# Last weight loads of a decode block in two pieces, with products of zeros ahead of TensorE's last pass

## The chip, the core and the metric

One core of one Trainium2 chip runs the whole kernel. The metric is the device time of one execution in microseconds. Weights come from HBM to SBUF by DMA, TensorE multiplies into PSUM, VectorE (DVE) and ScalarE (ACT) work on what TensorE leaves there, GpSimd (POOL) clears buffers, and SyncE (SP) issues the loads.

## The reference

One decode step for eight sequences of one token each, in f32: a pre-norm attention block over the last 1024 positions of a cache, then a gated feed-forward block, each with a residual.

```python
W  = min(4096, max(256, Sk // 4))                # 1024 of 4096 positions
q  = (layernorm(x) @ wq)                         # 8 x 4096, 32 heads of 128
s  = einsum(q, k_cache[last W]) * Dh ** -0.5     # 4 kv heads, each for 8 heads
o  = einsum(softmax(s), v_cache[last W]) @ wo
h  = x + o
g, u = layernorm(h) @ w_gate, layernorm(h) @ w_up    # 1024 x 3584 each
h2 = h + (gelu(g) * u) @ w_down                  # 3584 x 1024
```

Every weight is used once, so 111 MB are read for a result of 32 KB.

## The kernel before

**Tiles.** The activations are TensorE's stationary operand, 32 columns wide (eight tokens, each in every fourth column), and the weights stream past as the moving operand, 512 columns at a time. Four such products stand side by side in the four column groups of the array and write to four strips of 32 partitions in PSUM. `half(i, gates)` (L215) is one pass over a buffer: eight chunks `c`, each of four products (one per column group), the first four chunks into one half of `sums[i]`, the others into the other. A pass marks its middle and its end for the other engines.

**Buffers and loads.** There are two SBUF buffers of 8.4 MB. The twelve full loads (`units`, L151 to L156: wq, keys, values, wo, gate and up, two each) alternate between them, all on SP's queue, each issued when the pass that read the same buffer before it has ended. Then come the rest of `w_down` in row chunks of 128 rows (128 x 1024 f32, 0.52 MB each): 16 of them into buffer 0 in the pieces named by `PARTS` (L160, `wd0`, `wd1`, ...), three into buffer 1 by `ENDPARTS` (two, then one: the tails), and the last one as two blocks of columns by `ENDS` (160 and 96 of the 256 columns of a quarter: the ends).

**TensorE's order.** A loop of eight turns (L230) is written once. In a turn stand a pass `b` over buffer 1, two products with `y_sb` that fold four strips (L236; in most turns their result is not used), eight transposes of `source` (L241) that turn the last stage's result into the next stationary operand, and a pass `a` over buffer 0. Conditions leave out `b` in turns 1 and 4 and `a` in turn 3. Waits are counters that `take` lowers again (L209), so that the same code can wait in every turn: `go[0]` for a load and the operand of pass `a`, and `go_later` for gates inside pass `a`. GpSimd fills the gates' counters at the start with what the six earlier passes `a` will take (`GATE`, L197); in the last pass they hold it back for DVE's second operand (`go_0`, chunk 4) and for the later pieces of the loads (`go_1`, chunk 5; `go_2`, chunk 7). One chunk `c` of this last pass uses two row chunks.

**The end.** DVE adds the two halves of the last pass to the residual (`d1`, L423 and L424). TensorE then sums in PSUM's `acc`, by `quarters` (L427): the fold of pairs of strips (`add2` with `d1`) and the three row chunks of the tails (`chunk`, L434), in that order. ACT copies `acc` to `most` (L444). TensorE multiplies the two blocks of the last row chunk (L455), DVE adds each to `most` (`o_fin`, L458), and two DMAs write the result. Each engine works its queue strictly in the order written.

Of the kernel before, what the change touches and what calls it, by code (L numbers as in the profile page):

```python
# [7 lines left out]
P = 128  # L8
# [8 lines left out]
QW = D // NQ  # L17
N = 512
# [8 lines left out]
UNITS = 12  # L27
EARLY = 8
HEAD = 16
PARTS = (10, 4, 2)  # L30
ENDPARTS = (2, 1)
ENDS = (160, 96)
AHEAD = 3
PAD = 128


GATE = (1, 16, 16)
TURNS = 9
NO_B = (1, 4)
NO_A = (3,)  # L40


class Flow:
# [37 lines left out]
    def run(self, engine, make, *waits, mark=True, gives=None):  # L81
        ins = self.start(engine, make, waits)
        if gives is not None:
            ins.then_inc(*gives)
            return None
        if not mark:
            return None
        self.done[engine] += 1
        ins.then_inc(self.own[engine], 1)
        return self.own[engine], self.done[engine]  # L90
# [7 lines left out]
def decode_block(nc, x, units, dn, tails, ends, outs):  # L98

    fl = Flow(nc)  # L100
    run, move = fl.run, fl.move
    PE = nc.tensor
    scale = DH ** -0.5

    def sb(name, *shape):
        return nc.alloc_sbuf_tensor(name, list(shape), F32).ap()

    def bank(name, n):
        return nc.alloc_psum_tensor(name, [P, n], F32).ap()
# [5 lines left out]
    acc, fin = bank("acc", N), bank("fin", N)  # L115
# [3 lines left out]
    go = [fl.sem("go_a"), fl.sem("go_b")]  # L119
    go_later = [fl.sem(f"go_{i}") for i in range(len(GATE))]  # L120
    go_turn, go_fold = fl.sem("go_turn"), fl.sem("go_fold")
# [6 lines left out]
    for i in range(1, TURNS):  # L128
# [4 lines left out]
        nt += 1  # L133
        if i not in NO_A:
            seq += [("a", na, 0), ("a", na, 1)]
# [5 lines left out]
    def half_a(k, h=1):  # L141
        return at_mark["a", k, h]
# [8 lines left out]
    for u in range(UNITS):  # L151
        k, i = divmod(u, 2)
# [6 lines left out]
    q0 = EARLY  # L159
    for i, (n, sem) in enumerate(zip(PARTS, (go[0], *go_later[1:]))):  # L160
        c0 = (q0 - EARLY) * D
# [11 lines left out]
    last = q0  # L173
# [14 lines left out]
        pattern=[[-1, P]], channel_multiplier=1), z)  # L188
    y_sb = sb("y_sb", P, N)
    run("gpsimd", lambda e: e.memset(y_sb, 0.0), gives=(go_fold, 3))  # L190
    src_ok = run("gpsimd", lambda e: e.memset(source, 0.0))
    add2 = sb("add2", P, 2, 32)
    run("gpsimd", lambda e: e.tensor_add(
# [2 lines left out]
    for i, g in enumerate(go_later):  # L196
        run("gpsimd", lambda e: e.memset(note[:, i:i + 1], 0.0), gives=(g, GATE[i] * (passes - 1)))  # L197

# [10 lines left out]
    def take(sem, n):  # L209
        PE.wait_ge(sem, n).then_inc(sem, -n)  # L210

    def mark(ins):
        ins.then_inc(fl.own["tensor"], 1)

    def half(i, gates):  # L215
        gates = dict(gates)
        for c in range(NC):
            if c in gates:
                take(*gates[c])
            h = c // (NC // 2)  # L220
            for j in range(NQ):
                s = NQ * c + j
                ins = PE.matmul(  # L223
                    sums[i][32 * j:32 * j + 32, h * N:(h + 1) * N], still[i][:, 32 * s:32 * s + 32],
                    wbuf[i][:, s * N:(s + 1) * N],
                    start=(c % (NC // 2) == 0), stop=(c % (NC // 2) == NC // 2 - 1))
            if c % (NC // 2) == NC // 2 - 1:
                mark(ins)

    with PE.Fori(1, TURNS) as i:  # L230
        with PE.If(i != NO_B[0]):
            with PE.If(i != NO_B[1]):
                half(1, [(0, (go[1], 17))])
                take(go_fold, 1)
                for ch in range(2):
                    ins = PE.matmul(turned[0:32, ch * N:(ch + 1) * N], add2[:, ch, :], y_sb,  # L236
                                    start=True, stop=True)
                mark(ins)
        take(go_turn, 1)
        for n in range(NC):  # L240
            ins = PE.transpose(turned[:, n * P:(n + 1) * P], source[:, n * P:(n + 1) * P], ident)  # L241
        mark(ins)
        with PE.If(i != NO_A[0]):
            half(0, [(0, (go[0], 17)), *zip((4, 5, 7), zip(go_later, GATE))])
    fl.done["tensor"] = len(seq)


# [174 lines left out]
    d1 = sb("d1", P, N)  # L422
    tok = run("vector", lambda e: e.tensor_add(d1, rest, sums[0][:, 0:N]), tok, half_a(6, 0))  # L423
    d1_ok = run("vector", lambda e: e.tensor_add(d1, d1, sums[0][:, N:2 * N]), tok, half_a(6))  # L424


    def quarters(lhs, rhs, *waits, start=False, stop=False):  # L427
        for j in range(NQ):
            tok = run("tensor", lambda e: e.matmul(
                acc[32 * j:32 * j + 32, 0:QW], lhs(j), rhs(j), start=start, stop=stop),  # L430
                *waits, mark=(stop and j == NQ - 1))
        return tok

    def chunk(q, **flags):  # L434
        t, here = arrived[q]
        return quarters(lambda j: at[:, q, :], lambda j: t[:, j * QW:(j + 1) * QW], here, at_ok, **flags)

    quarters(lambda j: add2[:, j // 2, :], lambda j: d1[:, (j % 2) * QW:(j % 2) * QW + QW], d1_ok,
             start=True)
    chunk(last - 3)  # L440
    chunk(last - 2)
    tok = chunk(last - 1, stop=True)
    most = sb("most", P, QW)
    most_ok = run("scalar", lambda e: e.copy(most, acc[:, 0:QW]), tok)  # L444
# [8 lines left out]
    for (c0, n, t, here), d_ps in zip(blocks, (fin, sums[1])):  # L453
        for j in range(NQ):
            tok = run("tensor", lambda e: e.matmul(  # L455
                d_ps[32 * j:32 * j + 32, 0:n], at[:, last, :], t[:, j * n:(j + 1) * n],
                start=True, stop=True), here, d1_ok, mark=(j == NQ - 1))
# [103 lines left out]
```

## Time and profile before

| | |
|---|---|
| time, median of 3 runs | 263.79 us (263.63 to 263.81) |
| span of the profiled execution, first to last instruction | 262.3 us |
| median of the runs less this span | 1.5 us |
| TensorE busy | 138.9 us, 53% |
| DVE, ACT, POOL busy | 43.8, 13.5, 7.2 us |
| read from HBM | 111.18 MB, 424 GB/s over the span |
| packets on SP's load queue | 98.4% of the 16 DMA engines' span |

The profile gives no time of its own for that execution beside the span; the 1.5 us lie before the first and behind the last instruction. PE is TensorE, PEld its weight loads, which run beside the products. An f32 product stands in the trace as two records of PE, one behind the other. "PEq" means TensorE's own instruction sequencer, where the waits of `take` stand, so an idle time that ended with PEq includes waits for loads.

### The profile page before, as it was taken

The numbers are of one execution on the slowest core, as the hardware profiler recorded it, in microseconds if no ns is written. First come the engines' busy times: TensorE is split into PE (matmuls) and PEld (weight loads), VectorE is DVE, ScalarE is ACT, GpSimd is POOL, SyncE is SP. The second block draws the span as 40 slices with busy tenths as digits, with TensorE's granted clock in tenths as the row PEclk, the third lists the DMA queues.
The fourth block names the chain that finished last, engine by engine and source line by source line (L and its number), as shares of the span: only waits on it lengthen the run. The fifth ranks groups of instructions, "written<-read, shape, count | busy, mean of one in ns | idle before, by whom it ended". The sixth has DMA issues, their size and how long they took to land. (4 is left out here: it accounts for less than half of the span.)

```text
span 262.3 us, 2253 instructions
## 1 busy us (share of the span) xinstructions
PE 138.9 (53%) x968; PEld 43.5 (17%) x968; DVE 43.8 (17%) x115; ACT 13.5 (5%) x19; POOL 7.2 (3%) x18
## 2 busy tenths in 40 slices
PE   0025905916706937507908608629409809209985
PEld 0021201301102222102302102122102302002321
DVE  0340100240100140400410101263100300100422
ACT  1000000000030010000000200000300000200000
POOL 5000000100000000100100000000000000000000
PEclk9999965975975986965965957986966968957999
DMA  8998997999899799989979998997999999799895
GB/s 320 485 440 360 480 480 340 460 480 440 360 480 480 320 480 480 440 360 480 480 320 480 480 430 370 480 480 320 480 480 400 400 480 480 320 420 500 370 421 229
DMA packets 3040, 111.31 MB, mean 424 GB/s; under 512 B 472, under 2 KB 728, under 8 KB 992
## 3 DMA queue, kind: packets, MB, share of 16 engines
q1 hardware_dynamic: 2880, 111.23, 98.4%
q10 hardware_dynamic: 160, 0.08, 0.1%
HBM read 111.18 MB, written 0.13 MB: 424 GB/s over the span
## 5 line engine op out<-in xcount | busy, mean ns | idle before, releaser
L223 PE MATMUL sum<-w,still 128*32 128x512 f32 x832 | 115.7, 716 | 98.3 <-PEq L210 98.3
L223 PEld LDWEIGHTS sum<-w,still 128*32 128x32 f32 x832 | 31.9, 129 | 177.7 <-issue 177.7
L241 PE MATMUL turned<-ident,source 128*128 128x128 f32 x64 | 10.1, 310 | 21.1 <-PEq L210 21.1
L241 PEld LDWEIGHTS turned<-ident,source 128*128 128x128 f32 x64 | 8.0, 157 | 26.4 <-issue 26.4
L236 PE MATMUL turned<-y_sb,add 128*32 128x512 f32 x24 | 11.3, 592 | 0.9 <-PEq L210 0.9
L319 DVE TENSOR_REDUCE nmax<-sum 128x1 f32<-128x1024 f32 x2 | 2.4, 1224 | 30.1 <-PE sum L223 30.1
L394 DVE TENSOR_TENSOR up<-up,sum 128x512 f32<-128x512 f32 (+1 forms) x2 | 1.4, 686 | 36.3 <-PE sum L223 36.3
L290 DVE TENSOR_SCALAR q<-sum 128x512 f32<-128x512 f32 x2 | 1.4, 692 | 24.4 <-PE sum L223 24.4
L275 DVE COPY still<-turned 128x1024 f32<-128x1024 f32 x4 | 4.7, 1220 | 4.0 <-PE turned L241 4.0
L384 DVE TENSOR_TENSOR gate<-gate,sum 128x512 f32<-128x512 f32 (+1 forms) x2 | 1.4, 685 | 21.7 <-PE sum L223 21.7
L346 DVE SCALAR_TENSOR_TENSOR o<-sum,share,o 128x128 f32<-128x128 f32 x12 | 4.2, 351 | 4.2 <-PE sum L223 3.8
L343 DVE TENSOR_SCALAR o<-sum,share 128x128 f32<-128x128 f32 x2 | 0.7, 350 | 22.9 <-PE sum L223 22.9
L321 ACT ACT_TABLE_LOAD x1 | 1.3, 1283 | 59.4 <-DVE nmax L319 59.4
L236 PEld LDWEIGHTS turned<-y_sb,add 128*32 128x32 f32 x24 | 2.6, 110 | 8.7 <-issue 8.7
L350 POOL MEMSET still<- 128x1024 f32 x2 | 1.9, 951 | 76.0 <-PE sum L223 76.0
L362 DVE TENSOR_TENSOR y_sb<-y_sb,sum 128x512 f32<-128x512 f32 x1 | 0.7, 686 | 16.0 <-PE sum L223 16.0
L361 ACT COPY y_sb<-sum 128x512 f32<-128x512 f32 x1 | 0.6, 586 | 50.7 <-PE sum L223 50.7
L321 ACT ACTIVATE source<-sum,nmax 128x1024 f32<-128x1024 f32 x2 | 2.2, 1113 | 18.8 <-PE turned L241 18.8
L295 POOL MEMSET still<- 128x1024 f32 x2 | 1.9, 956 | 45.7 <-PE sum L223 45.7
L363 DVE TENSOR_TENSOR y_sb<-y_sb,sum 128x512 f32<-128x512 f32 x1 | 0.7, 689 | 14.1 <-PE sum L223 14.1
L306 DVE COPY still<-turned 128x16 f32<-128x16 f32 x32 | 2.7, 165 | 2.1 <-PE turned L241 2.1
L260 ACT ACT_TABLE_LOAD x2 | 2.6, 1283 | 3.0 <-POOL ident L186 2.9
(61 smaller groups left out, 38.8 us busy)
## 6 DMA issues: line engine op xcount, KB each, us to landing
w<-dn SPq DMA_DIRECT2D x1, 5120.0 KB, 22.9
w<-dn SPq DMA_DIRECT2D x1, 2048.0 KB, 27.4
w<-dn SPq DMA_DIRECT2D x1, 1024.0 KB, 29.4
w<-tails SPq DMA_DIRECT2D x1, 1024.0 KB, 12.8
w<-tails SPq DMA_DIRECT2D x1, 512.0 KB, 13.7
w<-ends SPq DMA_DIRECT2D x1, 320.0 KB, 14.1
w<-units SPq DMA_DIRECT2D x12, 29.5
w<-ends SPq DMA_DIRECT2D x1, 192.0 KB, 14.1
```

The source lines that it names most:

```text
L223: ins = PE.matmul(sums[i][32 * j:32 * j + 32, h * N:(h + 1) * N], still[i][:, 32 * s:32 * s + 32], wbuf[i][:, s * N:(s + 1) * N], start=(c ...
L236: ins = PE.matmul(turned[0:32, ch * N:(ch + 1) * N], add2[:, ch, :], y_sb, start=True, stop=True)
L241: ins = PE.transpose(turned[:, n * P:(n + 1) * P], source[:, n * P:(n + 1) * P], ident)
L260: tok = run("scalar", lambda e: e.activation(sd, ve, AF.Sqrt), tok)
L275: run("vector", lambda e: e.tensor_copy(still[i].rearrange("p (c j m) -> p c j m", c=NC, j=NQ), turned.rearrange("p (c m) -> p c m", c=NC) ...
L290: tok = run("vector", lambda e: e.tensor_scalar(q_sb, sums[hf][:, 0:N], scale, None, op0=ALU.mult), done(0, 0))
L295: cleared.append(run("gpsimd", lambda e: e.memset(still[hf], 0.0), done(0)))
L306: run("vector", lambda e: e.tensor_copy(to[:, :, b, s, a, REP * b:REP * b + REP].rearrange("p k (h i) -> p k h i", h=2), frm[:, s, a * HB ...
L319: tok = run("vector", lambda e: e.tensor_reduce(out=nmax, in_=sums[hf], axis=AX.X, op=ALU.max, negate=True), done(1))
L321: p_ok = run("scalar", lambda e: e.activation(source, sums[hf], AF.Exp, bias=nmax, accum_out=tot), tok, at_mark["t", 1 + hf])
L346: tok = run("vector", lambda e: e.scalar_tensor_tensor(out, o3[:, b], share[hf][:, b:b + 1], o_sb, op0=ALU.mult, op1=ALU.add), tok, done(2 ...
L350: cleared[hf] = run("gpsimd", lambda e: e.memset(still[hf], 0.0), done(2))
```

## The change

`PARTS` goes from (10, 4, 2) to (12, 4): the 16 row chunks come in two loads, the gates inside pass `a` are two and not three, and the second load is waited for at chunk 6 of the last pass. In the last turn, five products of a zeroed tile `idle` (128 x 32 by 128 x 512, into 32 partitions of the bank `fin`) stand between the transposes and pass `a`; GpSimd clears the tile at the start. Behind the loop, the fold of pairs stands behind the two row chunks of the first tail, no longer ahead of them.

```diff
-PARTS = (10, 4, 2)
+PARTS = (12, 4)
-GATE = (1, 16, 16)
+GATE = (1, 16)
+GATES = (4, PARTS[0] // 2)
+WARM = 5
...
+    idle = sb("idle", P, N)
+    run("gpsimd", lambda e: e.memset(idle, 0.0), mark=False)
     src_ok = run("gpsimd", lambda e: e.memset(source, 0.0))
...
         mark(ins)
+        with PE.If(i == TURNS - 1):
+            for _ in range(WARM):
+                PE.matmul(fin[0:32, 0:N], idle[:, 0:32], idle, start=True, stop=True)
         with PE.If(i != NO_A[0]):
-            half(0, [(0, (go[0], 17)), *zip((4, 5, 7), zip(go_later, GATE))])
+            half(0, [(0, (go[0], 17)), *zip(GATES, zip(go_later, GATE))])
...
-    quarters(lambda j: add2[:, j // 2, :], lambda j: d1[:, (j % 2) * QW:(j % 2) * QW + QW], d1_ok,
-             start=True)
-    chunk(last - 3)
+    chunk(last - 3, start=True)
     chunk(last - 2)
+    quarters(lambda j: add2[:, j // 2, :], lambda j: d1[:, (j % 2) * QW:(j % 2) * QW + QW], d1_ok)
     tok = chunk(last - 1, stop=True)
```

TensorE's instructions in the loop, from the transposes to the end of pass `a`, before (`x7` and the like count equal instructions; `go_a` is `go[0]`):

```order
L241 MATMUL turned<-ident,source 128x128 x7
L243 COMPARE_AND_BRANCH
L223 MATMUL sum<-w,still 32x512 [waits go_a_done]
L223 MATMUL sum<-w,still 32x512 x15
L223 MATMUL sum<-w,still 32x512 [waits go_0_done]
L223 MATMUL sum<-w,still 32x512 x3
L223 MATMUL sum<-w,still 32x512 [waits go_1_done]
L223 MATMUL sum<-w,still 32x512 x7
L223 MATMUL sum<-w,still 32x512 [waits go_2_done]
L223 MATMUL sum<-w,still 32x512 x3
```

The same place after the change (the lines of the code have moved by four and more):

```order
L245 MATMUL turned<-ident,source 128x128 x7
L247 COMPARE_AND_BRANCH
L249 MATMUL fin<-idle 32x512 x5
L247 UNCONDITIONAL_BRANCH
L250 COMPARE_AND_BRANCH
L227 MATMUL sum<-w,still 32x512 [waits go_a_done]
L227 MATMUL sum<-w,still 32x512 x15
L227 MATMUL sum<-w,still 32x512 [waits go_0_done]
L227 MATMUL sum<-w,still 32x512 x7
L227 MATMUL sum<-w,still 32x512 [waits go_1_done]
```

Five products and a condition now stand ahead of the wait for the first load; the wait at chunk 5 has moved to chunk 6 and the one at chunk 7 is gone.

TensorE behind the loop, before (`vector_done` is DVE's count, `we0` and `we1` the tails, `wl0` the first block of the ends):

```order
L429 MATMUL acc<-d,add 32x256 [waits vector_done]
L429 MATMUL acc<-d,add 32x256 x3
L429 MATMUL acc<-w,at 32x256 [waits we0_done]
L429 MATMUL acc<-w,at 32x256 x7
L429 MATMUL acc<-w,at 32x256 [waits we1_done]
L429 MATMUL acc<-w,at 32x256 x3
L455 MATMUL fin<-w,at 32x160 [waits wl0_done]
```

The same place after the change:

```order
L436 MATMUL acc<-w,at 32x256 [waits we0_done,vector_done]
L436 MATMUL acc<-w,at 32x256 x7
L436 MATMUL acc<-d,add 32x256 [waits vector_done]
L436 MATMUL acc<-d,add 32x256 x3
L436 MATMUL acc<-w,at 32x256 [waits we1_done]
L436 MATMUL acc<-w,at 32x256 x3
L461 MATMUL fin<-w,at 32x160 [waits wl0_done]
```

The fold with its wait for `d1` now stands between the two tails; the first tail's products carry a wait for an earlier DVE instruction, the copy to `at`.

## Rows read from the trace of the kernel before

**Rows 1.** Chain of waits that ended last: start, duration, what.
```profile
245.45 14.08 DMA w<-ends
...
260.47 0.25 DVE o_fin L458
```

**Rows 2.** Timeline of TensorE's products, last turn: start, duration, line, records, idle before.
```profile
235.55 8.99 PE L223 MATMUL sum<-w,still 128*32 128x512 f32 x64 [10.93 <-PEq L210]
244.35 1.88 PE L236 MATMUL turned<-y_sb,add 128*32 128x512 f32 x4
246.16 1.09 PE L241 MATMUL turned<-ident,source 128*128 128x128 f32 x8
247.67 4.50 PE L223 MATMUL sum<-w,still 128*32 128x512 f32 x40 [0.41 <-PEq L210]
252.57 1.92 PE L223 MATMUL sum<-w,still 128*32 128x512 f32 x16 [0.40 <-PEq L210]
255.05 1.06 PE L223 MATMUL sum<-w,still 128*32 128x512 f32 x8 [0.56 <-PEq L210]
256.92 0.64 PE L429 MATMUL acc<-d,add 128*32 128x256 f32 x8 [0.80 <-DVE d L424]
257.45 1.07 PE L429 MATMUL acc<-w,at 128*32 128x256 f32 x16
258.74 0.64 PE L429 MATMUL acc<-w,at 128*32 128x256 f32 x8 [0.21 <-DMA w<-tails]
259.57 0.48 PE L455 MATMUL fin<-w,at 128*32 128x160 f32 x8 [0.20 <-DMA w<-ends]
```

**Rows 3.** Timeline of DVE and ACT behind the last pass.
```profile
256.18 0.69 DVE L424 TENSOR_TENSOR d<-d,sum 128x512 f32<-128x512 f32 x1 [4.12 <-PE sum L223]
...
259.44 0.37 ACT L444 COPY most<-acc 128x256 f32<-128x256 f32 x1 [17.69 <-PE acc L429]
...
260.12 0.32 DVE L458 TENSOR_TENSOR o_fin<-most,fin 128x160 f32<-128x160 f32 x1 [1.19 <-PE fin L455]
260.47 0.25 DVE L458 TENSOR_TENSOR o_fin<-most,sum 128x96 f32<-128x96 f32 x1
```

**Rows 4.** Timeline of SP: the three loads of the 16 row chunks.
```profile
224.68 1.28 SPq L94 DMA_DIRECT2D w<-dn  x3
```

**Rows 5.** Costliest groups, the fold products: busy, mean ns of one, idle before.
```profile
L236 PE MATMUL turned<-y_sb,add 128*32 128x512 f32 x24 | 11.3, 592 | 0.9 <-PEq L210 0.9
```

**Rows 6.** Timeline of TensorE, an earlier turn: fold and transposes.
```profile
50.31 1.88 PE L236 MATMUL turned<-y_sb,add 128*32 128x512 f32 x4
52.13 1.09 PE L241 MATMUL turned<-ident,source 128*128 128x128 f32 x8
```

**Rows 7.** Timeline at the start: GpSimd's clearing, DVE's first use of `source`.
```profile
2.12 0.52 POOL L190 MEMSET y_sb<- 128x512 f32 x1
...
13.29 0.80 DVE L268 TENSOR_SCALAR source<-x_sb,ln_mv,ln_rs 32x1024 f32<-32x1024 f32 x1
```

**Rows 8.** Timeline of TensorE: three of its twelve full passes.
```profile
22.69 9.60 PE L223 MATMUL sum<-w,still 128*32 128x512 f32 x64 [6.51 <-PEq L210]
...
177.48 9.01 PE L223 MATMUL sum<-w,still 128*32 128x512 f32 x64 [1.47 <-PEq L210]
...
216.19 8.43 PE L223 MATMUL sum<-w,still 128*32 128x512 f32 x64 [7.06 <-PEq L210]
```

**Rows 9.** Windows: length, busy time (records) of PE, PEld, DVE, ACT, POOL; clock; DMA.
```profile
235.50:239.50 4.00, 3.95 (x20) 1.15 (x24) 0.00 (x0) 0.00 (x0) 0.00 (x0) 0.51 1.14 492
239.50:244.40 4.90, 4.90 (x49) 1.51 (x42) 0.00 (x0) 0.58 (x1) 0.00 (x0) 1.00 0.93 401
...
256.20:262.30 6.10, 3.07 (x48) 1.05 (x48) 1.36 (x6) 0.37 (x1) 0.00 (x0) 1.00 0.58 220
...
169.40:174.60 5.20, 0.28 (x3) 0.31 (x4) 4.26 (x10) 0.20 (x1) 0.00 (x0) 1.00 1.20 517
```

## What the change was expected to do

> **What bounds the kernel now.** I read the chain of waits first. It runs back from the last instruction through the ends of `w_down` and lasts from their issue at 245.45 until they land at 259.53; behind that come only TensorE's short products, DVE's two additions and the output [rows 1]. So the loads end last, not the arithmetic, and SP's queue is never empty: the three loads of the 16 row chunks are issued at 224.68 [rows 4], 23 us before the first of them is used.
>
> The second view is TensorE's timeline of the last turn [rows 2]. The last pass starts three times, at 247.67, 252.57 and 255.05, each time after a wait, because a load lands there. The starts give the stream's pace: four row chunks take 4.90 us and two take 2.48, so a row chunk costs 1.21 us and a transfer of its own 0.06. The tails follow in the same way at 257.45 and 258.74 and the first block of the ends at 259.57.
>
> The third view is what stands between the pass and the end on DVE and ACT [rows 3]. `d1` is added at 256.18, 1.13 us after the last chunk began; the fold starts 0.05 us after that addition. ACT's copy of `acc` runs from 259.44 to 259.81, and DVE's first `o_fin` waits until 260.12, for the last block's products. ACT's copy could end 0.26 us later (260.12 less 0.05 of handover less 259.81) before `o_fin` felt it. That is the slack of the arithmetic behind the loads, and it is small: only the copy's place decides it.
>
> **The change part by part.**
>
> *Two loads for three.* The bytes are the same. One transfer fewer is worth 0.06 us by the pace above, so tails and ends land 0.06 us earlier. SP issues two loads in place of three, 0.43 us less of 1.28 [rows 4], at a time when it has nothing else to do: nothing. The first load now holds twelve row chunks and lands two row chunks later, so the last pass can start at 247.67 + 2 x 1.21 = 250.09. The second is there at 255.05 - 0.06 = 254.99. A pass that began at 250.09 would need 0.86 us a chunk (below), reach chunk 6 at 255.24 and chunk 7 at 256.10, 1.05 us later than before.
>
> *Five products of zeros.* TensorE works in order, so they push the last pass back. Their nearest row is the fold: the same shape, 128 x 32 by 128 x 512 in f32, one column group, two records a product. Four records take 1.88 us, one lasts 0.592, so they follow each other every (1.88 - 0.592) / 3 = 0.429 us [rows 2, 5]. Ten records of zeros take 4.29 us. The ends of what is unknown are wide: a record cannot go much below the 0.136 us that one transpose of 128 columns takes on average (1.09 / 8, which makes 1.4 us for ten), and at TensorE's lower clock, at which a record takes twice as long, ten take 8.6 us. I take 4.29, because shape and clock agree with the row.
>
> They begin when the transposes leave the array. In an earlier turn the transposes, at 52.13, began 0.06 us before the modelled end of the fold at 52.19 [rows 6]; so here the zeros begin at 246.16 + 1.09 - 0.06 = 247.19 and the pass can begin at 251.48. Its load has been there since 250.09: the pass is 1.39 us late, and the loads don't start it any more.
>
> The pass itself: 40 records in 4.50 us are ten rounds of four, the last record again 0.59, so a round takes 0.43 and a chunk, two rounds, 0.86 [rows 2]. Chunk 6 begins at 256.64, long after its load at 254.99, and chunk 7 at 251.48 + 7 x 0.858 = 257.49, where it was 255.05: 2.44 us later.
>
> *The end of it.* `d1` starts 1.13 us behind, at 258.62, and ends at 259.31; the fold begins at 259.36. This is where its new place counts. TensorE has left the pass at 258.35 and does the two row chunks of the first tail (0.43 each, from 1.07 for two against 0.64 for one [rows 2]) while DVE adds: they end at 259.21, 0.15 before the fold can start. Ahead of them, the fold would have pushed all three row chunks back and cost another 0.86. Behind the fold, the last tail starts at 259.79; it landed an us before. ACT's copy starts 0.70 after it, as it did [rows 2, 3], at 260.49, and ends at 260.86; DVE's `o_fin` starts at 260.91 in place of 260.12. The blocks' products, 0.43 behind the tail at 260.22 and 0.55 long to `o_fin`, are ready before. The end moves by 0.79 us.
>
> *What costs nothing.* The cleared tile is a 0.52 us instruction on GpSimd like the one for `y_sb` [rows 7]; it pushes the clearing of `source` to about 4 us, and DVE first writes there at 13.29. Without that cover it would cost its 0.52. The added condition is read in every turn between transposes and pass `a`. The trace has no row for one; a condition's jump and a wait lie between fold and transposes, which shift by 0.10 against the fold's pace (50.31 + 4 x 0.429 = 52.03, then 52.13) [rows 6]. I take 0 for it, between 0 and 0.10 in each turn: before every pass TensorE waits, 1.47 us where it waits least [rows 8], and in the last turn the jump lies behind 4.29 us of queued zeros. The wait for the copy to `at` at the first tail is over ten us old when it is met.
>
> The sum is 263.79 + 0.79 = 264.58: the profiled execution's span is 262.3, the median of the runs lies 1.5 above, and I keep that distance.
>
> **The size that can move.** The chain starts from the pass over buffer 1 at 235.55, and the length of that pass depends on when TensorE's clock rises: in its first 4 us the granted clock is 0.51, the lower level of 1.2 GHz, and then 1.00, the upper one of 2.4 [rows 9]. Twelve passes of equal work last from 8.43 to 9.60 us [rows 8]; this one took 8.99 [rows 2]. Nothing ties it to that value in another execution. Before, that was hidden behind the load at 247.67; now it moves the end one for one: +0.79 becomes +0.23 to +1.40, that is 264.02 to 265.19.
>
> **The rivals.**
>
> *The stream still ends last: 263.73.* If the last pass begins by 251.48 - 0.79 = 250.69, the copy of `acc` is early enough, and only the 0.06 of the transfer is left. For it: three or four zeros would fit (247.19 + 4 x 0.858 = 250.62), so the count is just one too many; and a short pass over buffer 1 leaves only +0.23. Against it: five are written, and a record would have to take under 0.35 us where the fold's take 0.429. The Trainium skill (TensorE: Matmul & The Clock Gate, section Back-to-back issue gap) gives about 216 ns between isolated products of 512 columns at the upper clock; by that, an estimate, five zeros take 1.1 us, the pass starts with its load at 250.09, and the time is 263.73. The trace disagrees for f32 products of this shape, 0.86 us each, so I give that rule little.
>
> *The clock falls: 266.0 to 267.2.* If products of zeros in a quarter of the array did not hold the clock, the last pass would begin at the lower level like the one at 235.55. At the upper level a pass takes 15 x 0.43 + 0.59 = 7.04; the twelve took 8.43 to 9.60, so this adds 1.4 to 2.6 to 264.58. For it: the pass at 235.55 began at the lower level after a wait of 10.93 us [rows 2, 9]. Against it: it stayed at 1.00 to the end through the gaps of the last turn, and between 169.4 and 174.6, after nothing but a fold, with TensorE busy for 0.28 us of 5.2 [rows 9]. The Trainium skill (the same page, section Part 4: PE-mode transpose) says that transposes do not count as busy for the clock; if so the zeros, not the transposes, must hold it, and no run so far shows zeros alone.
>
> *Faster.* Every landing is 0.06 us earlier and no other work shrinks, so no row gives a gain beyond that.
>
> **How the numbers follow.** 0.2%, about what a measurement of this kernel can tell from no change, is 0.53 us: slower begins at 264.32. With the pass's length spread evenly over what the rows show, the shift lies over 0.53 in (1.40 - 0.53) / 1.17 = 74% of cases. I give 0.60 to TensorE's chain ending last and over that bound (264.58 the likeliest), 0.30 to an end inside it (the rest of that spread, shorter zeros, the stream), 0.06 to the fallen clock, 0.04 to a gain that no row shows. Slower 0.66, same 0.30, faster 0.04. The range for 8 in 10 runs from the stream's 263.7 to 265.3, a little over the longest pass.
>
> **What would show it.** In the profile after: ten records of zeros 0.43 apart from about 247.2; the last pass one piece without a wait from about 251.5, chunk 6 not waiting; `d1` near 258.6; the fold begun by DVE, not by a load; the chain of waits through TensorE, DVE and ACT's copy and no longer through the ends. If the zeros end by 250.7, or the last pass starts with its load, the sum is wrong and the stream decides; if the granted clock is under 1.00 behind 247, the third case holds. All times move with the length of the pass at 235.5, which is to be read first.

## The result, and the profile after

The changed kernel takes 265.08 us (median of 11 runs, 263.91 to 265.78) against 263.81 (11 runs, 263.58 to 264.18) for the kernel before: the ratio is 1.0040, 95% interval 1.0030 to 1.0049. It is 0.4% slower, twice the 0.2% at which the prediction let slower begin, and its runs lie 1.87 us apart where those of before lie 0.60 apart. The profiled execution has a span of 264.2 us; it took 265.47 us, 0.39 over the median.

The chain that ended last no longer has a load in it (start, duration, what); this answers to [rows 1].

```profile
235.99 9.57 PE sum L227 x64
245.57 1.69 PE turned L240 x4
247.26 1.02 PE turned L245 x8
248.28 3.98 PE fin L249 x9
...
252.69 6.25 PE sum L227 x60
...
259.56 1.94 PE acc L436 x26
261.50 0.02 issue
261.52 0.38 ACT most L450
```

It runs through TensorE from the pass over buffer 1 to the copy of `acc`, 26 us without one wait for a load. The timeline of TensorE's products shows the same pieces with their records, to be held against [rows 2].

```profile
248.21 4.05 PE L249 MATMUL fin<-idle 128*32 128x512 f32 x9
251.67 0.63 PE L227 MATMUL sum<-w,still 128*32 128x512 f32 x3
252.10 0.59 PE L249 MATMUL fin<-idle 128*32 128x512 f32 x1
252.13 7.00 PE L227 MATMUL sum<-w,still 128*32 128x512 f32 x60
258.56 0.61 PE L436 MATMUL acc<-w,at 128*32 128x256 f32 x6
258.96 0.59 PE L227 MATMUL sum<-w,still 128*32 128x512 f32 x1
259.39 1.03 PE L436 MATMUL acc<-w,at 128*32 128x256 f32 x10
260.38 0.64 PE L436 MATMUL acc<-d,add 128*32 128x256 f32 x8
260.84 0.61 PE L436 MATMUL acc<-w,at 128*32 128x256 f32 x8
```

No row of it has an idle time before it. The clock stood at its upper level through the zeros and the pass (windows: length, busy time of PE, PEld, DVE, ACT and POOL, then the clock, the DMA's share and GB/s):

```profile
248.20:252.10 3.90, 3.90 (x14) 1.06 (x17) 3.06 (x5) 0.00 (x0) 0.00 (x0) 1.00 0.74 315
252.70:259.50 6.80, 6.80 (x71) 2.07 (x64) 0.69 (x1) 0.00 (x0) 0.00 (x0) 1.00 0.96 392
```

DVE's part, against [rows 3], in the timeline of that engine:

```profile
259.64 0.69 DVE L431 TENSOR_TENSOR d<-d,sum 128x512 f32<-128x512 f32 x1 [2.75 <-PE sum L227]
...
262.00 0.32 DVE L464 TENSOR_TENSOR o_fin<-most,fin 128x160 f32<-128x160 f32 x1 [1.54 <-PE sum L461]
```

The fold still starts with DVE: `d1` ends at 260.33, and 0.05 us later the fold's weights are loaded, after a wait for it. The chain and the row of the products don't show this short wait, because the modelled ends of the tails' products cover it.

```profile
260.38 0.16 PEld L436 LDWEIGHTS acc<-d,add 128*32 128x32 f32 x8 [0.45 <-DVE d L431]
```

The tails and the ends landed, as in the page's list of loads (KB, us from issue to landing), 12.2, 13.1 and 13.4 us after issues that began at 245.62: the first block of the ends by 259.9, two microseconds before DVE could use it.

```profile
w<-tails SPq DMA_DIRECT2D x1, 1024.0 KB, 12.2
w<-tails SPq DMA_DIRECT2D x1, 512.0 KB, 13.1
w<-ends SPq DMA_DIRECT2D x1, 320.0 KB, 13.4
```

### The profile page after: what moved, and what is told of

The parts are those of the page before. It is cut to its first block, busy times and chain, and to the rows that moved or that the text cites. A ratio compares the mean times of both kernels' runs of the same rounds, so it can differ in the third digit from the quotient of the medians.

```text
span 264.2 us, 2274 instructions
## 1 busy us (share of the span) xinstructions
PE 144.7 (55%) x978; PEld 56.3 (21%) x978; DVE 43.7 (17%) x115; ACT 13.5 (5%) x19; POOL 7.7 (3%) x18
## 5 line engine op out<-in xcount | busy, mean ns | idle before, releaser
L227 PE MATMUL sum<-w,still 128*32 128x512 f32 x832 | 117.9, 721 | 95.2 <-PEq L214 95.2
L227 PEld LDWEIGHTS sum<-w,still 128*32 128x32 f32 x832 | 42.6, 130 | 166.1 <-issue 161.9
L245 PE MATMUL turned<-ident,source 128*128 128x128 f32 x64 | 11.0, 328 | 21.1 <-PEq L214 21.0
L245 PEld LDWEIGHTS turned<-ident,source 128*128 128x128 f32 x64 | 8.7, 167 | 26.4 <-issue 26.4
L249 PE MATMUL fin<-idle 128*32 128x512 f32 x10 | 4.5, 594 | 0.0
## 6 DMA issues: line engine op xcount, KB each, us to landing
w<-tails SPq DMA_DIRECT2D x1, 1024.0 KB, 12.2
w<-tails SPq DMA_DIRECT2D x1, 512.0 KB, 13.1
w<-ends SPq DMA_DIRECT2D x1, 320.0 KB, 13.4
w<-ends SPq DMA_DIRECT2D x1, 192.0 KB, 13.4
```

The lines of the kernel that those rows point to most:

```text
L227: ins = PE.matmul(sums[i][32 * j:32 * j + 32, h * N:(h + 1) * N], still[i][:, 32 * s:32 * s + 32], wbuf[i][:, s * N:(s + 1) * N], start=(c ...
L249: PE.matmul(fin[0:32, 0:N], idle[:, 0:32], idle, start=True, stop=True)
```

## The experiments

The theory: TensorE's own chain ends last, and its terms are the length of the pass over buffer 1, the ten records of zeros, the pass, and the fold's place. The rivals: the loads of 12 and 4 row chunks are what is slower; the zeros are needed because the clock falls without them. Times are medians; "before" is the old kernel run beside them.

**Without the zeros.**

```diff
-        with PE.If(i == TURNS - 1):
-            for _ in range(WARM):
-                PE.matmul(fin[0:32, 0:N], idle[:, 0:32], idle, start=True, stop=True)
```

> The changed kernel without the products of zeros. Theory (TensorE's chain, with the zeros in it, ends last): the last pass starts with its load, about 2.5 us behind the start it had before, chunk 7 runs from about 256.1 in the old kernel's time and d1 is ready near 257.9, so the stream ends last again: 263.7, with the small spread of the old kernel, provided the clock stays at 1.00. Rival (the load of twelve row chunks and its order make it slower, not the zeros): stays near 265. Rival (the zeros are needed for the clock): the granted clock falls in the 2.8 us of waiting and the last pass takes 1.4 to 2.6 us longer, which brings the end to 264.0 to 265.0.

264.82 us (264.75 to 264.93, 5 runs), before 263.77; ratio 1.0040 (1.0027 to 1.0054). My main expectation missed and the clock's rival was right. The last pass starts with its load, as the timeline of TensorE shows:

```profile
246.57 1.09 PE L242 MATMUL turned<-ident,source 128*128 128x128 f32 x8
250.22 8.77 PE L224 MATMUL sum<-w,still 128*32 128x512 f32 x64 [2.56 <-PEq L211]
```

but it takes 8.77 us where it could take 7.1. The windows of this kernel (length, busy time of PE and PEld, DVE, ACT, POOL, then the clock) say why:

```profile
247.70:250.20 2.50, 0.00 (x0) 0.01 (x1) 2.40 (x4) 0.00 (x0) 0.00 (x0) 1.00 0.57 243
250.30:253.80 3.50, 3.50 (x20) 1.16 (x23) 0.56 (x2) 0.00 (x0) 0.00 (x0) 0.51 1.00 426
253.80:259.00 5.20, 5.20 (x53) 1.89 (x48) 0.69 (x1) 0.00 (x0) 0.00 (x0) 1.00 0.98 395
```

After 2.5 us without a product the clock is at its lower level, and stays there until 253.8. So the changed loads with nothing in the wait cost 1.05 us. With zeros in the same place the clock stayed at 1.00 (the windows of the profile after): the zeros do hold it.

**Three zeros.**

```diff
-WARM = 5
+WARM = 3
```

> The changed kernel with three products of zeros, not five. Theory: 1.72 us less on TensorE, the zeros end near 249.8 for a pass over buffer 1 of 8.99 us and so ahead of the load at 250.1; chain at -0.93 against the old end where it was +0.79. So 263.7 in most runs, and up to 264.5 after the longest passes. Rival (the loads): stays near 265. Rival (each zero costs nothing because other column groups run beside it): stays near 265 as well.

263.67 us (263.46 to 264.24, 11 runs), before 263.77; ratio 0.9999 (0.9990 to 1.0008): no change that can be measured. The loads are those of the changed kernel, so as long as the clock is held they are not what is slower. The profiled execution had a long pass over buffer 1, and the last pass still began with its load in column groups 1 to 3; in group 0 the six records of zeros, 0.43 us apart, kept it back until about 250.48:

```profile
235.55 9.69 PE L227 MATMUL sum<-w,still 128*32 128x512 f32 x64 [10.22 <-PEq L214]
...
247.88 2.76 PE L249 MATMUL fin<-idle 128*32 128x512 f32 x6
250.08 7.44 PE L227 MATMUL sum<-w,still 128*32 128x512 f32 x64
```

The ends of `w_down` stand in its chain of waits again:

```profile
246.14 13.29 DMA w<-ends
```

**The zeros alone**, put into the old kernel.

```diff
+WARM = 5
...
+    idle = sb("idle", P, N)
+    run("gpsimd", lambda e: e.memset(idle, 0.0), mark=False)
...
+        with PE.If(i == TURNS - 1):
+            for _ in range(WARM):
+                PE.matmul(fin[0:32, 0:N], idle[:, 0:32], idle, start=True, stop=True)
```

> The old kernel with nothing but the five products of zeros put in. Theory: the pass is as late as in the changed kernel (d1 done near 259.3 for a pass over buffer 1 of 8.99 us), but the fold stands ahead of all three row chunks of the tails, so these come 0.86 us later: the end at +1.65 against the old kernel, +0.86 against the changed one, 265.5 to 266.0 with the spread of the changed kernel. Rival (the loads of 12 and 4 made it slower): 263.8 as the old kernel.

265.98 us (265.24 to 266.38, 5 runs), before 263.77; ratio 1.0084 (1.0069 to 1.0099). As the theory had it: the zeros alone make the old kernel slower by more than the whole change does, since the fold's old place is still behind them. TensorE's rows:

```profile
259.62 0.64 PE L435 MATMUL acc<-d,add 128*32 128x256 f32 x8 [0.83 <-DVE d L430]
260.08 1.48 PE L435 MATMUL acc<-w,at 128*32 128x256 f32 x24
```

All 24 records of the tails, whose loads had landed by 258.80, come behind the fold.

**The clock held through the pass over buffer 1.**

```diff
+AHEAD_B = 11
...
             with PE.If(i != NO_B[1]):
+                with PE.If(i == TURNS - 1):
+                    for _ in range(AHEAD_B):
+                        PE.matmul(fin[0:32, 0:N], idle[:, 0:32], idle, start=True, stop=True)
                 half(1, [(0, (go[1], 17))])
```

> The changed kernel with eleven more products of zeros in the last turn, ahead of the wait for the load of the pass over buffer 1, where TensorE waits 10.9 us. They take 9.4 us and end before that load lands. Theory (the length of this pass, set by when the clock rises, moves the end one for one): the pass runs at the upper level throughout, 7.1 us in place of 8.4 to 10, TensorE's chain is 1.9 us shorter, and the stream ends last: 263.7 with the small spread of the old kernel, five zeros still in place. Rival (the spread of the changed kernel comes from the loads): spread and median stay, 264 to 265.8. Rival (products of zeros do not hold the clock): the pass begins at the lower level and the time stays near 265.

264.79 us (264.64 to 264.87, 5 runs), before 263.77; ratio 1.0039 (1.0025 to 1.0053). Half of the expectation held: the five runs lie within 0.23 us, and the pass ran at the upper level.

```profile
226.54 9.60 PE L240 MATMUL fin<-idle 128*32 128x512 f32 x22
236.67 7.07 PE L228 MATMUL sum<-w,still 128*32 128x512 f32 x64 [0.53 <-PEq L215]
```

But its load came at 236.5 and not at 235.5, the last pass again waited for its load, at 251.25, and the chain of waits ran through the tails. The queues of this kernel show a third line that those of the kernels so far do not have:

```profile
q8 instruction: 1, 0.02, 0.0%
```

It is one packet of 16 KB, at 19.4 us, and it took 0.94 us. The trace has sixteen landing marks for a load, and a load is there with the last of them. In every load behind the packet these lie 1.6 us apart (234.92 to 236.54 for the pass over buffer 1) where they lay 0.44 apart in the kernel before; fifteen of them come by 235.43, as they did there, and a single one 1.1 us behind. The two kernels that follow take this apart.

**The same with a shorter program.**

```diff
+AHEAD_B = 11
...
+                with PE.If(i == TURNS - 1):
+                    with PE.Fori(0, AHEAD_B):
+                        PE.matmul(fin[0:32, 0:N], idle[:, 0:32], idle, start=True, stop=True)
```

> As the run before with the clock held (eleven products of zeros in the last turn ahead of the pass over buffer 1), but written as one product in an inner loop of eleven turns, so that TensorE's program grows by few instructions. In that run the pass took 7.07 us at clock 1.00, yet every load landed about 1.1 us later than in the changed kernel, after one 16 KB fetch of instructions at 19.4 us. Theory 1 (the program's length caused the fetch and the fetch the late stream; the pass's length moves TensorE's chain): no fetch behind the start, loads on time, last pass waiting for its load at 250.1, 263.7 with a spread of about 0.4. Theory 2 (zeros ahead of the pass, or TensorE kept busy, slow the loads): landings 1.1 us late again, 264.8. Theory 3 (the spread of the changed kernel has nothing to do with this pass): 264 to 265.8.

263.64 us (263.52 to 264.25, 11 runs), before 263.75; ratio 1.0000 (0.9991 to 1.0009). Five zeros are still in place ahead of the last pass, and neither the loss nor the spread is left (0.73 us between the runs, 0.63 for the kernel before beside them). The pass over buffer 1 takes 7.07 us, the zeros end before the load, and the last pass waits for it:

```profile
235.54 7.07 PE L228 MATMUL sum<-w,still 128*32 128x512 f32 x64 [0.30 <-PEq L215]
...
245.23 4.48 PE L253 MATMUL fin<-idle 128*32 128x512 f32 x10
250.07 7.07 PE L228 MATMUL sum<-w,still 128*32 128x512 f32 x64 [0.36 <-PEq L215]
```

The windows show the clock through zeros and both passes:

```profile
226.00:235.50 9.50, 9.24 (x22) 2.20 (x20) 0.99 (x2) 1.64 (x2) 0.00 (x0) 1.00 0.96 414
235.60:242.60 7.00, 7.00 (x65) 2.51 (x66) 0.00 (x0) 0.58 (x1) 0.00 (x0) 1.00 1.04 449
247.00:250.00 3.00, 2.71 (x7) 0.53 (x5) 1.46 (x3) 0.00 (x0) 0.00 (x0) 1.00 1.01 431
250.00:257.00 7.00, 6.93 (x64) 2.38 (x64) 0.69 (x1) 0.00 (x0) 0.00 (x0) 1.00 0.96 403
```

This is the strongest single test of the theory: the changed kernel's loss goes when a term 10 us ahead of the zeros shrinks from 9.57 us, in the profile after, to 7.07.

**Code that is never run**, in the old kernel.

```diff
             with PE.If(i != NO_B[1]):
+                with PE.If(i == TURNS + 1):
+                    for _ in range(20):
+                        PE.matmul(fin[0:32, 0:N], y_sb[:, 0:32], y_sb, start=True, stop=True)
                 half(1, [(0, (go[1], 17))])
```

> The old kernel with twenty products under a condition that never holds, at the head of the loop: TensorE's program grows by these, nothing more is executed. Theory (a longer program needs one more fetch of instructions through the DMA engines that carry the loads, and the stream never makes the delay good): one 16 KB instruction packet near 20 us, the landings of a load spread over 1.5 us in place of 0.45, the end 1.0 to 1.2 us later, 264.9. Rival (what slowed the stream was the execution of zeros): 263.8.

264.80 us (264.68 to 264.92, 5 runs), before 263.75; ratio 1.0040 (1.0027 to 1.0054). The instruction packet is there again, this time at 7.2 us and 0.93 us long, the sixteen marks of a load lie 1.5 us apart, again with a single one behind, and the ends land 1.0 later in the chain of waits:

```profile
247.29 13.22 DMA w<-ends
260.52 0.04 issue
```

So in the run with the clock held it was the length of TensorE's program that delayed the loads, not the zeros' execution; the short loop stood at the same place in the program and delayed nothing. That the packet is the link is read from the traces: of the ten profiles these two have it, and only in these two does one mark of every load come 1.1 us behind the rest. Which DMA engine carried the packet is not shown.

**The loads of 12 and 4 alone**: the changed kernel without zeros, with the fold back ahead of the tails, here against the old kernel.

```diff
-PARTS = (10, 4, 2)
+PARTS = (12, 4)
-GATE = (1, 16, 16)
+GATE = (1, 16)
+GATES = (4, PARTS[0] // 2)
...
-            half(0, [(0, (go[0], 17)), *zip((4, 5, 7), zip(go_later, GATE))])
+            half(0, [(0, (go[0], 17)), *zip(GATES, zip(go_later, GATE))])
```

> The old kernel with the loads of 12 and 4 row chunks alone: no zeros, the fold ahead of the tails as before. Theory: as in the run without zeros the clock falls in the wait for the first load, d1 is done near 259.7 and the fold starts then; all three row chunks of the tails stand behind it, 0.86 us later than in that run: 265.7. Rival (the fold's place is worth nothing, since the chunks wait for their loads anyway): 264.8.

265.62 us (265.43 to 265.88, 5 runs), before 263.75; ratio 1.0067 (1.0054 to 1.0081). Against the run without zeros the fold's place is worth 0.80 us (265.62 - 264.82), near the 0.86 of two chunks that TensorE could do while DVE adds.

**The fold's place alone**, in the old kernel.

```diff
-    quarters(... d1 ..., d1_ok, start=True)
-    chunk(last - 3)
+    chunk(last - 3, start=True)
     chunk(last - 2)
+    quarters(... d1 ..., d1_ok)
     tok = chunk(last - 1, stop=True)
```

> The old kernel with the fold moved behind the two row chunks of the first tail alone. Theory: the fold was done before the tails landed and has 0.2 us of room between them in its new place, so the stream ends last as before: 263.8. Rival (the last tail's products come later behind the fold): up to 264.1.

263.73 us (263.61 to 264.16, 11 runs), before 263.75; ratio 1.0001 (0.9992 to 1.0010). Where the stream ends last, the move is free and worth nothing:

```profile
257.63 1.07 PE L429 MATMUL acc<-w,at 128*32 128x256 f32 x16 [1.42 <-DMA w<-tails]
258.49 0.64 PE L429 MATMUL acc<-d,add 128*32 128x256 f32 x8
258.92 0.64 PE L429 MATMUL acc<-w,at 128*32 128x256 f32 x8
```

No version here beats the old kernel: with three zeros, or with the clock held by the short loop, it is level with it.

## Why the prediction was right, point by point

**The direction and the mechanism** held: TensorE's chain took the place of the stream, and the fold was begun by DVE, one of the signs that the prediction named. In the profile after, everything from the transposes on is 1.03 us later than the prediction's times (transposes at 247.19 against 246.16), and with that shift taken off the steps fall on their marks: zeros at 248.21 - 1.03 = 247.18 (247.19 predicted), `d1` at 258.61 (258.62), the fold at 259.35 (259.36), ACT's copy at 260.49 (260.49), `o_fin` at 260.97 (260.91).

**The ten records** of zeros followed each other every 0.43 us, as the fold's row had it [rows 5]. The rival by the Trainium skill (TensorE: Matmul & The Clock Gate, section Back-to-back issue gap), 216 ns a product of 512 columns, did not hold for these f32 products.

**The size** came out larger: +1.27 us between the medians where the sum had +0.79. The sum took two terms at the value that one execution had, and in the profile after both were larger: the pass over buffer 1 lasted 9.57 where the prediction had 8.99, and it began with its load at 235.99 where the prediction had 235.55. The 0.58 and the 0.44 make up the 1.03. These are not the shares of the median run, of which there is no trace. Over the eight profiles in which nothing held the clock ahead of this pass it lasted 8.58 to 9.78 us, 9.26 on average; with that length the prediction's sum would have been +1.06, an estimate.

The range for 8 in 10 runs held 8 of the 11; the other three (265.47, 265.52 and 265.78) all lie above its 265.3. The spread behind it was too narrow. The twelve passes of [rows 8] hold, within 0.05 us, only three lengths that repeat (9.60, 8.47, 9.04, then 9.59, 8.46, 9.01 and so on to the end). Another execution has another three, such as 8.60, 9.17 and 9.73 in the kernel with three zeros, and the longest full pass in any profile, in the kernel with the clock held, is longer than all of [rows 8]:

```profile
62.52 10.00 PE L228 MATMUL sum<-w,still 128*32 128x512 f32 x64 [7.19 <-PEq L215]
```

That the length of this pass decides over the loss was argued from rows; the run with the clock held by a short loop shows it. How the spread of the runs divides between this length and the landing of its load stays open.

**The point from which it decides**, a last pass that begins by 250.69, agrees with the runs on either side of it. With three zeros group 0 of the pass was free at about 250.48, behind a pass over buffer 1 of 9.69 us. ACT's copy then ended at 259.85, where the prediction's sum puts it for such a start (259.86), `o_fin` waited for the ends until 260.02, and the time was 263.67 where the stream's case had 263.73. No run lies between 250.48 and the 252.53 of the profile after, so the point itself is worked out and not shown. That case's 0.06 us for a transfer less is too small to be shown by these intervals.

**The fold's new place** was priced at 0.86; 0.80 was measured where TensorE's chain ends last, nothing where the stream does.

**The fallen clock** did not come true with zeros in place, and I had weighed it for the wrong kernel. The prediction let a pass that began with its load at 250.09 run at 0.86 us a chunk even without zeros, and the expectation of the first experiment repeated this. The wait that the load of twelve brings is long enough for the clock to fall, and that costs 1.05 us, nearly the 1.27 of the whole change. The trace of before already had such a fall. The prediction's reading against it, the clock at 1.00 from 169.4 to 174.6 with TensorE hardly busy [rows 9], stops where the clock drops: the next 2.8 us are at the lower level, and the transposes there take 1.69 us where those of [rows 6] take 1.09.

```profile
174.32 1.69 PE L241 MATMUL turned<-ident,source 128*128 128x128 f32 x8 [4.96 <-PEq L210]
174.60:177.40 2.80, 1.41 (x8) 1.01 (x6) 1.35 (x2) 0.00 (x0) 0.09 (x1) 0.50 0.87 375
```

The rule that transposes do not count as busy (the Trainium skill, the same page, Part 4: PE-mode transpose) is tested by no run here. Without zeros the eight transposes at 246.57 did not keep the clock up past 250.3, but 2.5 us of waiting stood behind them, so this does not show whether they counted for less than products would have.

## What to carry to other kernels

Products that keep TensorE's clock up are work in its queue like any other (five here cost 1.27 us, three cost nothing): count them so that they end when the awaited data lands, and from the latest start that the work ahead of them can have, since whatever they overshoot goes into the end. A kernel bound by loads hides the spread of TensorE's passes; a change that uses up the slack shows that spread in the time, so the slack is to be worked out against the longest pass seen in several executions, not the one in the profile. A window with the clock still up does not show that a wait is free for the clock: read the stretch behind it too. And before adding code to an engine in a loop, see whether the trace gains an instruction packet.

## What the runs showed of the hardware that was not expected

**A longer program delayed the loads for the rest of the run.** Twenty products that never run added one 16 KB instruction packet, and from then on one of the sixteen landing marks of every load came 1.1 us behind the others; the ends landed 1.0 us later, and so did the end of the kernel. Eleven products that do run brought the same packet, at 19.4 us. The stream of loads is never idle here, and in neither run was the delay made good. Five products more, or eleven in an inner loop beside these five, brought no packet. Where between these the limit lies was not tried.

**Column groups ran ahead of each other.** In the profile after, three products of the last pass (column groups 1 to 3) start at 251.67, ahead of the last record of zeros in group 0 at 252.10, whose product stands before them in the program; likewise six records of the tails start at 258.56, ahead of the pass's last record at 258.96. The lead over that record was 0.43 us, one record. So the section on the kernel before says too much where it has each engine work strictly in the order written: between column groups the records shift. It saved nothing here, because group 0 had its own row of products to finish.
